# Which queues carry the two sliding layers' loads and the constant rows, and how many token buffers there are, in a four-layer attention kernel

## The chip, the cores and the metric

The kernel runs on one core of a Trainium2 chip. The core has a matrix engine (PE in the profile, with its weight loads shown apart as PEld), a vector engine (DVE), a scalar engine (ACT), a general engine (POOL) and an engine that only issues transfers (SP). Every engine works through its own instructions in order. ACT and POOL can issue DMA transfers from their own instruction streams too; a transfer that is issued so stands in line with the engine's other work. The metric is device time in microseconds (us) of one whole execution, as the median of several runs.

## The reference

```python
x = A_x                                             # 1 x 2048 tokens x 512, float32
x = x + A(layernorm(x), A_wqkv, A_wo)               # layer 0: sliding window of 256
x = x + B(layernorm(x), B_wqkv, B_wo)               # layer 1: full attention
x = x + A(layernorm(x), A_wqkv, A_wo)               # layer 2: as layer 0
x = x + B(layernorm(x), B_wqkv, B_wo)               # layer 3: as layer 1

# A and B, with 32 heads of 16
q, k, v = split(x @ wqkv)
p = softmax(q @ k.T / 4)          # A: only keys j with 0 <= i - j < 256
return (p @ v) @ wo
```

## The kernel before

The tokens are cut into four chunks of 512 (NQ = 4, QC = 512), and the 32 heads into eight groups of four (a group is `qd` in the code). For every layer, chunk and group the kernel makes scores on PE (line 675), exponentials of them on ACT (line 679), in the sliding layers sets the entries outside the window to zero on POOL (lines 742 and 745), and multiplies by the values on PE (line 719 in the full layers, 752 in the sliding ones). A sliding layer's group takes three steps, a full layer's sixteen. The product of one step is issued on PE two steps after its scores.

The work of projecting, normalizing and so on is called side work and is woven into the attention steps. `project` makes keys and queries (matmuls at line 387 in the sliding layers), ACT and DVE bring the result to two float16 halves (lines 495 and 498), and SP stores them to scratch tensors in DRAM (`kw` for sliding keys, `kf` for full keys, `qs` for queries; lines 508 to 512). A further row of each query, made on DVE as `m` or `m_None`, is stored at line 554. Other rows of these scratch tensors are constant ones or zeros; `fill` (lines 262 to 269) writes them. Before a group's scores, its part of the keys and queries is read back from DRAM: `load_win` (lines 700 to 709) for a sliding layer, with two transfers a group in the first chunk and three in the others, and `load_full` (lines 688 to 698) for a full one. The tiles that hold them, `kt` and `qt`, have three buffers each. A group's load is issued in the program one group before its use.

`load_x` (line 440) fetches four tiles of 128 tokens from DRAM into the tag `x`, which has XB buffers. In `wo` the result of the output projection is added to such a tile (line 617), the tile is stored (line 618) and its statistics and normalization follow on DVE (lines 406 to 432). The normalized tile `xh` is written transposed into `xc` by a transposing DMA on SP (line 453, `transposed`); the projections of the next layer read `xc`. `NN` does the same for the first layer's chunks 2 and 3 and `T` names the transposes. `weights` (line 348) fetches prepared weights from DRAM into two buffers.

The order on PE is written out by the program: the `Side` class decides with an estimated clock which piece of side work goes between which attention steps. The order on the other engines, SP and the issuing streams included, comes from the framework's scheduler, which places the instructions by priority and by when it expects them to be ready; the window's zeroing has a raised priority. The framework also chooses the semaphores. The trace names the semaphore on which each transfer's landing is counted: in this kernel eight of them serve all transfers, and SP and ACT take them in turn from the same eight. A transfer that is to use one waits until the transfer before it on that semaphore has landed, whichever of the two engines issued it.

`fill` is called at the start for chunk 0 (lines 1038 and 1039) and later through `F` (line 1071), a piece of side work, for the other chunks of layer 0 and for the scratch of the full layers. The calls through `F` make 21 transfers: two for each of the three key chunks and one for each of the three query chunks of the sliding layers, eight for the full layers' keys and four for their queries.

Of the kernel before, what the change touches and what calls it, by code (L numbers as in the profile page):

```python
# [18 lines left out]
S, D, H, DH, WIN = 2048, 512, 32, 16, 256  # L19
# [5 lines left out]
QC = 512  # L25
# [5 lines left out]
SCALE = DH ** -0.5  # L31
MM = 0.222
HEAD_START = 100
EB, XB, XNB, WB, VB, OB = 6, 5, 4, 2, 3, 5
RUN = 4
L_MIN = 2.0 ** -90
L_SUM = 2.0 ** 60
# [141 lines left out]
def interleave_kernel(tc, *args):  # L179
    nc = tc.nc  # L180
    with tc.tile_pool(name="flag", bufs=1) as fp:
        flag = fp.tile([1, 1], I32, name="flag")
        fast_path(tc, flag, *args)
        good = nc.values_load(flag, min_val=0, max_val=P)
        with tc.If(good < P):
            general_path(tc, *args)
# [3 lines left out]
def fast_path(ctx, tc, flag, a_x, a_wqkv, a_wo, b_wqkv, b_wo, out):  # L190
# [3 lines left out]
    nc = tc.nc  # L194
# [25 lines left out]
    def wait(us):  # L220
# [9 lines left out]
    ones = cp.tile([P, QC], F16, name="ones")  # L230
# [3 lines left out]
    zeros = cp.tile([P, QC], F16, name="zeros")  # L234
# [3 lines left out]
    kw = [dp.tile([NP, P, QC], F16, name=f"kw{c}") for c in range(NQ)]  # L238
    kf = dp.tile([NP, P, S], F16, name="kf")
    qs = {(ty, c): dp.tile([NP, P, QC], F16, name=f"qs{ty}_{c}") for ty in range(2) for c in range(NQ)}  # L240
# [11 lines left out]
                            fill=0.0, base=0, channel_multiplier=1)  # L252
    nc.gpsimd.affine_select(hsum, hsum, pattern=[[DH, 32]], compare_op=ALU.is_ge,
                            fill=0.0, base=DH - 1, channel_multiplier=-1)
# [4 lines left out]

    def fill(t, key, c0=0, c1=1):
        r4 = lambda d0, d1: rows(t).rearrange("h (d b) (c n) -> h d b c n", b=4, n=QC)[:, d0:d1, 3]
        for c in range(c0, c1):
            if key:
                nc.sync.dma_start(r4(0, 1)[:, 0, c], ones[:H])
                nc.sync.dma_start(r4(1, DH)[:, :, c], zeros[:H, None, :].broadcast_to([H, DH - 1, QC]))
            else:
                nc.sync.dma_start(r4(1, DH)[:, :, c], ones[:H, None, :].broadcast_to([H, DH - 1, QC]))


    def load_w(ty, s, tag="vf", n="wr", behind=None):
        raw = wp.tile([P, NC, D], F32, name=f"{n}{ty}_{s}", tag=tag, bufs=VB if tag == "vw" else NQ)
        if behind is not None:
            nc.vector.tensor_copy(raw[:, 0, :1], behind)
        if s < 3:
            nc.sync.dma_start(raw, mats[ty, s].rearrange("(k p) f -> p k f", p=P))
        else:

            for u in range(2):  # L280
                for h in range(4):
                    nc.sync.dma_start(raw[32 * h + DH * u:32 * h + DH * u + DH],
                                      mats[ty, s].rearrange("(k u h d) f -> u h d k f", u=2, h=4, d=DH)[u, h])
        return raw
# [413 lines left out]
        return kts, qt  # L698

    def load_win(l, c, qd):  # L700
        n = f"{l}_{c}_{qd}"
        kt = pp.tile([P, 2, S // 2], F16, name=f"kt{n}", tag="kt", bufs=3)
        qt = pp.tile([P, 2, QC], F16, name=f"qt{n}", tag="qt", bufs=3)
        pair = slice(2 * qd, 2 * qd + 2)
        nc.scalar.dma_start(qt, qs[0, c][pair].rearrange("r p n -> p r n"))
        nc.scalar.dma_start(kt[:, :, WIN:WIN + QC], kw[c][pair].rearrange("r p n -> p r n"))
        if c:
            nc.scalar.dma_start(kt[:, :, :WIN], kw[c - 1][pair, :, QC - WIN:].rearrange("r p n -> p r n"))
        return kt, qt

    def attn_full(l, c, qd, kt, qt, a):
# [323 lines left out]
    xs = load_x(0, 0)  # L1035
    xT = XC[0, 0] = wp.tile([P, 2, NC, QC], F16, name="xc0_0", tag="xc", bufs=NQ)
    raw = {m: load_w(0, m, "xc") for m in (1, 0, 2)}
    fill(kw[0], True)
    fill(qs[0, 0], False)
    for i in range(4):  # L1040
        stats(0, 0, i, xs[i])
    mv = ST[0, 0][1]
# [28 lines left out]
    def F(parts):  # L1071

        def gen():
            for p in parts:
                fill(*p)
                yield wait(8)
        return Work(gen(), 0.0, None, aside=True)
# [101 lines left out]
```

## Time and profile before

| | |
|---|---|
| median of three runs | 2735.25 us (2733.8 to 2735.88) |
| the profiled execution's own time | 2728.47 us |
| its span, first to last instruction | 2726.8 us |
| mean granted TensorE clock | 0.987 |
| PE busy | 2603.9 us, 95% |
| ACT busy | 2375.5 us, 87% |
| DVE busy | 852.7 us, 31% |
| POOL busy | 518.9 us, 19% |

All times inside the execution are us from the first instruction. Layer 0's attention runs from about 65 to 425 us, layer 1 from about 476, layer 2 from about 1440 to 1715, layer 3 from about 1760 to the end. A row of the timeline has the start, the duration, the engine, the line, the operation, the tile written and the tiles read, the shape and the count; in brackets the idle time of the engine before it and what ended it. An engine's name with a q (SPq, ACTq) is its issuing stream. A row of the waits has who waited, for whom, the total in us, how often, and the longest.

### The profile page before, as it was taken

How to read it: one execution, taken by the hardware profiler on the slowest of the kernel's cores; microseconds unless marked ns; L12 is line 12 of the kernel's file. 1: busy time of each engine (PE TensorE's matmuls, PEld its weight loads, DVE VectorE, ACT ScalarE, POOL GpSimd, SP SyncE). 2: the span in 40 equal slices, each digit the busy share in tenths (PEclk: the TensorE clock that was granted, in tenths of full speed). 3: DMA queues.
4: the chain of work that ended last, by engine and by line, in shares of the span. 5: the costliest groups of instructions: out<-in, count | busy, mean ns of one | idle time of the engine just before them, and what ended most of it. 6: DMA issues, size and time to landing. Idle time of an engine off the chain costs nothing.

```text
span 2726.8 us, 59387 instructions
## 1 busy us (share of the span) xinstructions
PE 2603.9 (95%) x24315; PEld 752.5 (28%) x24315; DVE 852.7 (31%) x1949; ACT 2375.5 (87%) x2683; POOL 518.9 (19%) x1154
## 2 busy tenths in 40 slices
PE   7798999999999999999999989899999999999998
PEld 3233344222222222222223333422222222222221
DVE  6565554013243113112216566311222221121111
ACT  4675664999999999999997767499999999999997
POOL 0465661000000000000006678100000000000000
PEclk9899999999999999999999999999999999999999
DMA  7898666234353223212325565523334333333331
GB/s 240 240 278 254 194 196 208 78 101 114 112 122 100 69 77 109 86 61 92 100 73 172 177 170 149 166 78 95 114 112 129 121 114 104 104 104 121 97 96 52
DMA packets 322715, 353.14 MB, mean 130 GB/s; under 512 B 114433, under 2 KB 234497, under 8 KB 316417
## 3 DMA queue, kind: packets, MB, share of 16 engines
q1 hardware_dynamic: 270336, 308.35, 37.3%
q10 hardware_dynamic: 52096, 40.91, 5.1%
q8 instruction: 192, 3.15, 0.5%
q14 instruction: 91, 0.74, 0.1%
HBM read 236.45 MB, written 96.99 MB: 122 GB/s over the span
## 4 chain that ended last, share of the span: by engine, by line
PE 77%; ACT 8%; DVE 7%; issue 5%; DMA 3%; SPq 1%; POOL 0%; ACTq 0%; DVEq 0%; POOLq 0%
PE acc L719 30%; PE s L675 20%; PE b L387 10%; PE acc L384 10%; ACT e L679 7%; PE acc L752 5%; PE bs L387 1%; DMA xc<-xh 1%; DVE ot L647 1%; DVE wa L321 1%; DVE xh L432 1%; DMA x<-in_A_x_dram 1%; DVE xn L426 0%; DVE xh L426 0%; DVE st L406 0%
## 5 line engine op out<-in xcount | busy, mean ns | idle before, releaser
L679 ACT ACTIVATE e<-s 128x1024 f32<-128x1024 f32 (+2 forms) x2432 | 2245.7, 1115 | 176.2 <-PE s L675 128.9
L719 PE MATMUL acc<-e,vt 128*17 128x512 f32 x8192 | 1080.4, 599 | 5.0 <-DVE ot L647 4.0
L675 PE MATMUL s<-qt,kt 64*128 64x512 f16 (+3 forms) x5504 | 771.4, 356 | 41.8 <-ACT e L679 23.2
L675 PEld LDWEIGHTS <-kt 64*128 64x128 f16 x5504 | 198.4, 94 | 785.6 <-issue 763.5
L745 POOL TENSOR_SCALAR_AFFINE_SELECT e<-e 128x256 f32<-128x256 f32 x512 | 231.2, 459 | 125.8 <-ACT e L679 124.9
L719 PEld LDWEIGHTS acc<-e,vt 128*17 128x17 f32 x8192 | 136.3, 95 | 385.6 <-issue 352.9
L647 DVE STREAM_TRANSPOSE ot<-acc 128x512 f32<-128x512 f32 x128 | 91.5, 715 | 447.9 <-PE acc L719 334.6
L742 POOL TENSOR_SCALAR_AFFINE_SELECT e<-e 128x256 f32<-128x256 f32 x448 | 196.9, 445 | 97.9 <-ACT e L679 94.0
L752 PE MATMUL acc<-e,vt 128*17 128x384 f32 (+2 forms) x2816 | 197.2, 395 | 0.0
L387 PE MATMUL b<-xc,w 128*128 128x512 f16 x676 | 164.4, 385 | 27.1 <-DMA xc<-xh 14.3
L663 POOL TENSOR_TENSOR oh<-o,oh 128x512 f16<-128x512 f32 x31 | 36.0, 1160 | 719.8 <-DVE oh L662 656.6
L387 PEld LDWEIGHTS <-w 128*128 128x128 f16 x800 | 72.5, 99 | 143.8 <-issue 61.2
L384 PE MATMUL acc<-xc,w_h 128*32 128x512 f16 x1296 | 108.5, 379 | 2.3 <-DVE km L536 2.3
L384 PE MATMUL acc<-xc,w 128*32 128x512 f16 x1344 | 108.9, 379 | 1.7 <-DVE sp L498 0.9
L604 POOL TENSOR_SCALAR vt<-vt 128x16 f32<-128x16 f32 (+1 forms) x96 | 24.5, 256 | 441.8 <-DVE vt L602 288.2
L497 DVE TENSOR_SCALAR sp_h<-acc 128x512 f16<-128x512 f32 x27 | 18.6, 690 | 282.0 <-PE acc L384 282.0
L635 DVE SCALAR_TENSOR_TENSOR x<-acc,x 128x512 f32<-128x512 f32 x60 | 41.5, 692 | 206.1 <-PE acc L384 206.1
L384 PE MATMUL acc<-wo,oh 128*32 128x512 f16 x1296 | 102.2, 382 | 3.3 <-DVE m_None L548 3.3
L497 DVE TENSOR_SCALAR sp<-acc 128x512 f16<-128x512 f32 x28 | 19.3, 688 | 270.7 <-PE acc L384 257.4
L503 POOL TENSOR_TENSOR sq_h<-sp_h 128x512 bf16<-128x512 f16 x27 | 28.1, 1040 | 388.5 <-DVE sp_h L497 388.5
L602 DVE COPY vt<-acc 128x256 f32<-128x256 f32 (+1 forms) x36 | 18.5, 514 | 264.3 <-PE acc L384 264.3
L387 PE MATMUL b<-wo,oh 128*128 128x512 f16 x390 | 97.0, 385 | 3.0 <-DMA wo<-wd 3.0
(134 smaller groups left out, 1537.8 us busy)
## 6 DMA issues: line engine op xcount, KB each, us to landing
kt<-kf SPq DMA_DIRECT2D x128, 512.0 KB
xd<-x SPq DMA_DIRECT2D x96, 256.0 KB
x<-xd SPq DMA_DIRECT2D x96, 256.0 KB
w<-wd SPq DMA_DIRECT2D x20, 1024.0 KB
kt<-kw ACTq DMA_DIRECT2D x64, 256.0 KB
qt<-qs ACTq DMA_DIRECT2D x64, 256.0 KB
qt<-qs SPq DMA_DIRECT2D x64, 256.0 KB
qs<-sp SPq DMA_DIRECT2D x48, 256.0 KB
```

The lines of the kernel that those rows point to most:

```text
L384: nc.tensor.matmul(ps[g:g + 32], a[:, g:g + 32], b, start=(i == 0), stop=(i == len(pairs) - 1), skip_group_check=True)
L387: nc.tensor.matmul(ps, a, b, start=(go and i == 0), stop=(i == len(pairs) - 1))
L497: nc.vector.tensor_scalar(sp[:, 0], ps, e, None, op0=ALU.mult)
L635: nc.vector.scalar_tensor_tensor(xs[i], ps, 1.0 / (UP[2] * UP[3]), xs[i], op0=ALU.mult, op1=ALU.add)
L647: nc.vector.transpose(ot.rearrange("p b r -> p (b r)"), a)
L663: (nc.gpsimd if l % 2 and (l, c, qd) != (3, NQ - 1, NQD - 1) else nc.vector).tensor_tensor(hl[:, 1], o, hl[:, 0], ALU.subtract)
L675: nc.tensor.matmul(ps[:, h, s0:s0 + wd_], kt[R * h:R * h + R, pr, kc:kc + P], qt[R * h:R * h + R, pr, qc:qc + wd_], start=True, stop=True)
L679: nc.scalar.activation(e[:, :, w0:w1], ps[:, :, w0:w1], AF.Exp, scale=SCALE)
L719: nc.tensor.matmul(a[32 * h:32 * h + DH + 1, :], V[l, qd // 4, j // 8][:, j % 8, 4 * (qd % 4) + h, :], es_[h // 2][:, h % 2, :], start=(j ...
L742: nc.gpsimd.affine_select(v, v, pattern=[[0, 2], [-1, P]], compare_op=ALU.is_gt, fill=0.0, base=0, channel_multiplier=1)
L745: nc.gpsimd.affine_select(v, v, pattern=[[0, 2], [1, P]], compare_op=ALU.is_ge, fill=0.0, base=0, channel_multiplier=-1)
L752: nc.tensor.matmul(a[32 * h:32 * h + DH + 1, q * P:(q + nb) * P], V[l, (4 * c + j) // 4][:, j % 4, 4 * qd + h, :], es_[h // 2][:, h % 2, s ...
```

## The change

Three things are changed. The loads of the sliding layers' keys and queries, which ACT issued in both, are issued by POOL in layer 0 and by SP in layer 2. The constant rows are written through POOL, apart from the two calls for chunk 0 at the start, which stay on SP. The tag `x` has six buffers where it had five.

```diff
-EB, XB, XNB, WB, VB, OB = 6, 5, 4, 2, 3, 5
+EB, XB, XNB, WB, VB, OB = 6, 6, 4, 2, 3, 5
...
-    def fill(t, key, c0=0, c1=1):
+    def fill(t, key, c0=0, c1=1, q=nc.gpsimd):
         r4 = lambda d0, d1: rows(t).rearrange("h (d b) (c n) -> h d b c n", b=4, n=QC)[:, d0:d1, 3]
         for c in range(c0, c1):
             if key:
-                nc.sync.dma_start(r4(0, 1)[:, 0, c], ones[:H])
-                nc.sync.dma_start(r4(1, DH)[:, :, c], zeros[:H, None, :].broadcast_to([H, DH - 1, QC]))
+                q.dma_start(r4(0, 1)[:, 0, c], ones[:H])
+                q.dma_start(r4(1, DH)[:, :, c], zeros[:H, None, :].broadcast_to([H, DH - 1, QC]))
             else:
-                nc.sync.dma_start(r4(1, DH)[:, :, c], ones[:H, None, :].broadcast_to([H, DH - 1, QC]))
+                q.dma_start(r4(1, DH)[:, :, c], ones[:H, None, :].broadcast_to([H, DH - 1, QC]))
...
     def load_win(l, c, qd):
-        n = f"{l}_{c}_{qd}"
+        n, q = f"{l}_{c}_{qd}", nc.sync if l else nc.gpsimd
         kt = pp.tile([P, 2, S // 2], F16, name=f"kt{n}", tag="kt", bufs=3)
         qt = pp.tile([P, 2, QC], F16, name=f"qt{n}", tag="qt", bufs=3)
         pair = slice(2 * qd, 2 * qd + 2)
-        nc.scalar.dma_start(qt, qs[0, c][pair].rearrange("r p n -> p r n"))
-        nc.scalar.dma_start(kt[:, :, WIN:WIN + QC], kw[c][pair].rearrange("r p n -> p r n"))
+        q.dma_start(qt, qs[0, c][pair].rearrange("r p n -> p r n"))
+        q.dma_start(kt[:, :, WIN:WIN + QC], kw[c][pair].rearrange("r p n -> p r n"))
         if c:
-            nc.scalar.dma_start(kt[:, :, :WIN], kw[c - 1][pair, :, QC - WIN:].rearrange("r p n -> p r n"))
+            q.dma_start(kt[:, :, :WIN], kw[c - 1][pair, :, QC - WIN:].rearrange("r p n -> p r n"))
         return kt, qt
...
-    fill(kw[0], True)
-    fill(qs[0, 0], False)
+    fill(kw[0], True, q=nc.sync)
+    fill(qs[0, 0], False, q=nc.sync)
```

## The prediction

> **What bounds the kernel now.** I read the page first, then who waited on PE, then the two sliding stages as windows, then the issuing streams around each stall.
>
> ```profile
> span 2726.8 us, 59387 instructions
> ...
> PE 2603.9 (95%) x24315; PEld 752.5 (28%) x24315; DVE 852.7 (31%) x1949; ACT 2375.5 (87%) x2683; POOL 518.9 (19%) x1154
> ...
> PE 77%; ACT 8%; DVE 7%; issue 5%; DMA 3%; SPq 1%; POOL 0%; ACTq 0%; DVEq 0%; POOLq 0%
> ```
>
> PE carries 77% of the chain. The change touches the two sliding layers, so only these two stretches can move (the sixth buffer reaches further, below):
>
> ```profile
> core 0: us, PE busy (x) PEld busy (x) DVE busy (x) ACT busy (x) POOL busy (x), PEclk, DMA share, GB/s
> 65.00:425.00 360.00, 322.89 (x2922) 127.12 (x2920) 202.18 (x473) 232.13 (x300) 207.66 (x496) 0.95 0.78 229
> 1440.00:1715.00 275.00, 256.61 (x2643) 98.32 (x2636) 172.04 (x418) 194.49 (x230) 200.15 (x490) 0.98 0.58 173
> ```
>
> In layer 0 PE is idle for 360 - 322.9 = 37.1 us and in layer 2 for 18.4 us. That is the most that better transfers can win. No other engine is full: POOL has 360 - 207.7 = 152.3 us left in layer 0. Which waits make up the 37 us:
>
> ```profile
> PE b L387 <- DMA xc<-xh: 14.3, 1, 14.3
> ...
> PE s L675 <- ACT e L679: 9.9, 10, 3.3
> PE b L387 <- DMA w<-wd: 9.9, 1, 9.9
> ```
>
> Two single stalls and ten small ones. The first is the largest. PE waits for the transposed tokens of chunk 2:
>
> ```profile
> 104.03 1.04 PE L387 MATMUL b<-w,xc 128*128 128x512 f16 x4
> 119.38 1.87 PE L387 MATMUL b<-xc,w 128*128 128x512 f16 x4 [14.31 <-DMA xc<-xh]
> ```
>
> DVE had the last of these tokens ready at 77.99 + 0.77 = 78.8 and the last query half that SP stores ahead of them at 84.28 + 0.69 = 85.0:
>
> ```profile
> 77.99 0.77 DVE L432 TENSOR_TENSOR xh<-xn,xh 128x512 f16<-128x512 f32 x1
> ...
> 84.28 0.69 DVE L498 SCALAR_TENSOR_TENSOR sp<-b,sp 128x512 f16<-128x512 f32 x1 [3.14 <-ACT sp L495]
> ```
>
> But SP issued the transposes from 101.28 to 117.25 only:
>
> ```profile
> 100.42 0.34 SPq L512 DMA_DIRECT2D qs<-sp  x1
> ...
> 101.28 4.59 SPq L453 DMA_TRANSPOSE xc<-xh  x2
> 105.98 2.76 SPq L554 DMA_DIRECT2D qs<-m_None  x4
> ...
> 110.20 0.43 SPq L269 DMA_DIRECT2D qs<-ones  x1
> 110.67 6.58 SPq L453 DMA_TRANSPOSE xc<-xh  x2
> ```
>
> What kept SP is in its own waits, from 60 to 310 us:
>
> ```profile
> SPq L511 <- DMA qt<-qs: 11.0, 3, 5.6
> ...
> SPq L512 <- DMA qt<-qs: 6.6, 1, 6.6
> SPq L282 <- DMA qt<-qs: 5.5, 1, 5.5
> ```
>
> A store of chunk 1's queries and a load of raw weights do not use the `qt` that ACT fetched. The link is the completion semaphore: SP and ACT take the same eight in turn, and the next user waits until the last one's transfer has landed. Since ACT issues its load only between exponentials, SP inherits ACT's lateness, 23.1 us in these three rows. The reverse holds too: ACT's loads wait for SP's transposes, and its exponentials stand behind them:
>
> ```profile
> 301.87 0.37 ACTq L706 DMA_DIRECT2D kt<-kw  x1
> 302.28 0.60 ACT L600 ACTIVATE vt<-b 128x512 f32<-128x512 f32 x1 [6.10 <-DMA xc<-xh]
> ```
> ```profile
> 161.06 0.49 PE L675 MATMUL s<-qt,kt 64*128 64x384 f16 x4 [2.10 <-ACT e L679]
> ```
> ```profile
> 303.84 0.39 PE L675 MATMUL s<-qt,kt 64*128 64x256 f16 x4 [3.30 <-ACT e L679]
> ```
> ```profile
> 1632.21 0.49 PE L675 MATMUL s<-qt,kt 64*128 64x256 f16 x4 [2.85 <-ACT e L679]
> ```
>
> These three are the largest of PE's waits for ACT in the two layers.
>
> **The change part by part.** *Layer 0's loads leave ACT.* ACT gives up 88 issues of layer 0 (two for each of 8 groups in chunk 0, three for each of 24) and with them the shared semaphores. Without ACT's loads ahead of them SP's last query store goes at about 86, the transposes follow. At the pace of the slower pair above (3.3 us each) four take 13 us, to about 99; the last landed 2 us after its issue ended (117.25 to 119.4), so at about 101. PE asks at 104.03 + 1.04 = 105.1. So the 14.3 us go, with 4 us to spare, and with them 0.8 us of the slow first matmuls (1.87 against 1.04 for four in the rows above). Bounds: -15.1 and 0, the latter if the saturated DMA engines bring the transposes as late as before; I take -15. The two waits for ACT in layer 0 go, 2.1 + 3.3 = -5.4. Late next after the first stall is the `w` load of the second:
>
> ```profile
> 240.48 0.35 SPq L445 DMA_DIRECT2D x<-in_A_x_dram  x1
> 240.92 0.38 SPq L348 DMA_DIRECT2D w<-wd  x1
> ```
>
> It stands on SP behind a token load that waits for a buffer until DVE's normalization; I leave its 9.9 us as they are.
>
> *They arrive on POOL.* There 88 loads and the 21 constant-row transfers become 109 issues in line with the window's zeroing:
>
> ```profile
> L745 POOL TENSOR_SCALAR_AFFINE_SELECT e<-e 128x256 f32<-128x256 f32 x256 | 116.8, 463 | 88.2 <-ACT e L679 87.8
> L742 POOL TENSOR_SCALAR_AFFINE_SELECT e<-e 128x256 f32<-128x256 f32 x224 | 100.6, 454 | 66.6 <-ACT e L679 64.8
> ```
>
> No POOL issue is in this trace. The nearest rows are ACT's issue (median 0.40 us, longest 2.20) and a full-tile operation on POOL (1.16 us):
>
> ```profile
> L706 ACTq DMA_DIRECT2D kt<-kw x64: 366/395/2202, 28.8 to 1683.3; - x64
> ```
> ```profile
> L663 POOL TENSOR_TENSOR oh<-o,oh 128x512 f16<-128x512 f32 x31 | 36.0, 1160 | 719.8 <-DVE oh L662 656.6
> ```
>
> I take 1.1 us, near the row of the same engine, and 0.4 and 2.2 as ends. 109 x 1.1 = 120 us against 152.3 idle, or 132 if 20 us of stalls vanish: it fits, nearly full. The zeroing is late by up to three issues in a row, 3.3 us. What hides that is the two-step distance between a score and its product; that PE hardly waits for POOL today shows in
>
> ```profile
> PEld acc L752 <- POOL e L742: 4.4, 18, 0.4
> ```
>
> At 0.25 us a group the remainder costs 32 x 0.25 = +8 us, an estimate. Ends: 0 at 0.4 us (44 us of issue, well hidden) and, at 2.2 us, 207.7 + 240 = 447 us of POOL in a stage of 360, +87.
>
> The page "SBUF — State Buffer" of the Trainium skill (its part on the two sides of SBUF) speaks against this move: descriptors for POOL's transfers are written by POOL's own cores, which VectorE's two-port operations lock out, 0.62 us alone becoming 3.1 us beside one. By an estimate from that page, 109 issues would cost 68 us alone, which fits, and 338 us if every one were so hit, which does not. The kinds of operation that the page names are few here: twenty normalizing passes of this form in the whole stage, 12.1 us together.
>
> ```profile
> L426 DVE TENSOR_SCALAR xn<-x,mv,y 128x512 f32<-128x512 f32 x20 | 12.1, 604 | 0.3
> ```
>
> So I expect few such hits; no issue of POOL's in this trace shows one.
>
> *Layer 2's loads go to SP.* ACT loses 88 issues of 0.4 us, all beside PE's work, and the 2.85 us at 1632 go: -3. SP takes 88 x 0.4 = 35 us of 275. What they now stand behind is a store that waits for DVE:
>
> ```profile
> SPq L618 <- DVE x L617: 79.7, 16, 13.4
> ```
>
> With three buffers a load may start when the group three before has made its scores, two groups ahead of its use. A group of three steps takes 275 / 32 = 8.6 us, so it has 17 us, and the longest wait of 13.4 still leaves 3.8 for 1.2 us of issue and 2 of landing. Where SP's chain is itself late, at the three inner chunk ends, some 1.2 us of issue come on top: between 0 and 4, I take +2.
>
> *Constant rows and the sixth buffer.* SP loses 21 issues of 0.4 us, in the first stall 0.43 us at 110.20; it is in the sum already. The sixth buffer lets one more token tile be fetched ahead, but a chunk has four and the fourth still waits for an older one to be normalized; 0, between -5 (the `w` load at 240.92 no longer behind it) and 0. In the full layers, where ACT is nearly always busy, it changes nothing.
>
> **The sum.** -15 - 5.4 + 8 - 3 + 2 = -13.4. The profiled execution took 2728.47, so 2715.1; it was 6.8 us below the median of the runs, 2735.25, against which the forecast stands: 2735.25 - 13.4 = 2722.
>
> **The rivals.** *POOL becomes the bound* (slower). Layer 0 holds POOL 207.7 us; with 109 issues it fills 360 us at (360 - 207.7) / 109 = 1.4 us each. Beyond that every 0.1 us costs 11 us. At 1.6 us, halfway from 1.16 to 2.2, POOL needs 382 us: +22, and 2757. For it: POOL works at 58% already, and each group's loads come in threes ahead of its zeroing. Against: the row of its own full-tile work is under 1.4.
>
> *The stall comes back* (no change). For it, the DMA engines are nearly full just there:
>
> ```profile
> 103.00:119.00 16.00, 2.07 (x20) 0.49 (x14) 2.65 (x6) 2.47 (x3) 3.05 (x7) 0.72 0.98 243
> 119.00:150.00 31.00, 28.79 (x240) 9.42 (x242) 25.86 (x61) 23.57 (x34) 20.18 (x44) 0.89 0.92 309
> 150.00:253.00 103.00, 88.95 (x792) 34.92 (x788) 56.34 (x127) 63.67 (x82) 56.17 (x135) 0.93 0.92 274
> ```
>
> The change moves no byte away; what PE gains at 105 it could lose by 253 to the same bytes. Then only the small waits remain to pay for POOL: -8.4 + 10 = +2, 2737. Against: at 243 GB/s the stall's stretch moved less than the next one's 309, so it was short of issue rather than of bandwidth. The page "DMA: Bandwidth & Descriptors" of the Trainium skill (its part "Issuing engines are not separate DMA queues") says that issuing from another engine saves only issue time; by it the change is worth nothing on PE's path, this rival's time. The trace's SP waits for `qt` say that here a queue also holds others up.
>
> *Layer 2's loads come late on SP.* The margin of 3.8 - 3.2 = 0.6 us is gone where a second store's wait, at the mean of 79.7 / 16 = 5.0 us, stands ahead of the same load: 4.4 us late, and once a chunk 4 x 4.4 = +18, so 2740. For it: SP's queue is in order, and the stores come four to a chunk. Against: their waits follow PE's own order, which the loads follow as well.
>
> **How the numbers follow.** The forecast has 0.58, POOL as the bound 0.22, the returning stall 0.12, late loads on SP 0.08. A measurement here tells 0.2%, 5.5 us, from no change. Faster is the forecast and a third of the returning stall: 0.62; same is the rest of that and half of the late loads: 0.12; slower 0.26. The forecast's own range is 2705 (all gains with the 5 us of the `w` load, POOL free: 2735 - 30) to 2730. For eight in ten it goes from 2703 up through most of the POOL rival, to 2762 (1.64 us an issue).
>
> **What would show it.** Right: no `DMA qt<-qs` among SP's waits in layer 0, transposes of chunk 2 issued before 95, PE's 14.3 us wait for `xc` gone, POOL's busy time in layer 0 up to about 330 us with issue rows near 1.1 us, and PE's idle time there at 25 us or less. Wrong: POOL issues over 1.4 us, PE's waits for POOL's zeroing of more than 1 us each, or SP's transposes still after 100. The prediction fails most easily in the price of one POOL issue.

## The result, and the profile after

The changed kernel took 2720.89 us (median of five runs, 2717.27 to 2722.7) against 2733.83 us (2730.97 to 2735.88) of the kernel before in the same comparison: a ratio of 0.9951 with a 95% interval of 0.9937 to 0.9966, or 13 us. A second comparison of the same two kernels gave 2719.3 against 2727.58 us, 0.9964 (0.9951 to 0.9977), or 8 us. The profiled execution after took 2722.56 us; the one before, 2728.47 us, was a low one, so the two traces differ by less than the medians do.

The head of the page after, and the two sliding stages as windows:

```profile
span 2720.6 us, 59477 instructions
...
PE 2599.0 (96%) x24315; PEld 751.6 (28%) x24315; DVE 859.3 (32%) x1949; ACT 2376.8 (87%) x2683; POOL 592.2 (22%) x1263
```
```profile
core 0: us, PE busy (x) PEld busy (x) DVE busy (x) ACT busy (x) POOL busy (x), PEclk, DMA share, GB/s
65.00:425.00 360.00, 325.87 (x2944) 128.78 (x2942) 202.62 (x456) 235.58 (x304) 265.52 (x586) 0.97 0.76 221
1440.00:1715.00 275.00, 258.18 (x2643) 99.18 (x2636) 175.72 (x420) 195.31 (x231) 202.89 (x490) 0.98 0.61 176
```

In layer 0 PE's idle time went from 37.1 to 360 - 325.9 = 34.1 us only, while POOL's work rose by 57.9 us to 265.5. In layer 2 the window hides the gain, because its fixed ends take in other work; the stage has to be cut at its own first and last product. That is the table to read this case by. Its times are the starts of rows of line 752 in each timeline, in us:

```
                         first product  layer 0  layers 0->2  layer 2  from there
                         of layer 0     to last  (layer 1)    to last  to the end
before                       70.7        352.7     1023.3      265.2     1014.9
after                        73.8        349.6     1022.6      258.7     1015.9
```

The first product came 3.1 us later, layer 0 took 3.1 us less, and so both end at 423.4 us: in this pair of traces all that was won in layer 0 was lost ahead of it. The 6.5 us of layer 2 make up the difference of the spans, 6.2 us. The last column holds the same instructions in every kernel, and over the fourteen traces of this case it took anything from 1013.6 to 1021.2 us; a few us between two spans therefore say little, and the columns of the sliding layers and the medians of many runs are what to go by.

What the prediction said of SP and of the first stall is there. SP's waits from 60 to 310 us no longer name `qt` or `kt`. The two longest groups are stores that wait for DVE's result and weight loads that wait for PE:

```profile
SPq L511 <- DVE sp L498: 33.0, 9, 10.8
SPq L348 <- PE s L675: 24.9, 4, 12.7
```

The trace shows the link itself too: in the changed kernel POOL's 109 transfers are counted on eight semaphores of their own, and no transfer of SP's or ACT's is counted on one of these. The transposes of chunk 2 go out from 89.41 us on instead of 101.28, and PE's wait there, 14.31 us before, is 2.26 (the profile names nothing that ended it):

```profile
89.41 7.13 SPq L453 DMA_TRANSPOSE xc<-xh  x2
96.65 3.04 SPq L554 DMA_DIRECT2D qs<-m_None  x4
...
100.13 7.13 SPq L453 DMA_TRANSPOSE xc<-xh  x2
```
```profile
110.90 1.02 PE L387 MATMUL b<-xc,w 128*128 128x512 f16 x4 [2.26 <-issue]
...
126.63 1.87 PE L387 MATMUL b<-xc,w 128*128 128x512 f16 x4 [5.33 <-DVE sp L498]
...
130.59 0.39 PE L675 MATMUL s<-qt,kt 64*128 64x256 f16 x2 [2.09 <-ACT e L679]
...
161.18 0.61 PE L675 MATMUL s<-qt,kt 64*128 64x128 f16 x4 [10.59 <-ACT e L679]
...
246.88 3.46 PE L387 MATMUL b<-xc,w 128*128 128x512 f16 x8 [4.49 <-DMA w<-wd]
```

But three new waits stand behind it, 5.33 + 2.09 + 10.59 = 18 us where there had been 2.1. The two of 2.09 and 10.59 us are for ACT. It was not held by a load of keys now, but by the preparation of layer 1's weights, which waits in ACT's order for raw weights, with the exponentials behind it:

```profile
127.66 2.19 ACT L290 ACTIVATE w<-wr 128x512 f16<-128x512 f32 x4 [8.27 <-DMA wr<-in_B_wqkv_dram]
...
159.07 1.15 ACT L290 ACTIVATE w<-wr 128x512 f16<-128x512 f32 x2 [8.54 <-DMA wr<-in_B_wqkv_dram]
```

SP issued these two loads at 111.96 and 145.50 us; before, the first was issued at 121.73, and ACT came to its tile at 132.27 without a wait. In the order that ACT now has, the preparation stands ahead of exponentials that could run, while its own data is not there. The wait of 5.33 us is another one. It is for DVE, whose line 498 stood behind statistics that waited for token loads:

```profile
121.30 0.69 DVE L406 BATCH_NORM_STATS2 st<-x 128x6 f32<-128x512 f32 x1 [2.54 <-DMA x<-in_A_x_dram]
...
125.95 0.63 DVE L498 SCALAR_TENSOR_TENSOR sp<-b,sp 128x512 f16<-128x512 f32 x1
```

POOL's issue is the term that the prediction was least sure of. By operation and tile (busy us, mean ns of one):

```profile
L705 POOL DMA_DIRECT2D qt<-qs x32 | 23.7, 740 | 23.2 <-PE s L675 14.6 <-DMA qs<-m_None 8.0 <-issue 0.3
L706 POOL DMA_DIRECT2D kt<-kw x32 | 23.2, 725 | 24.4 <-DMA kw<-sp 24.2
L708 POOL DMA_DIRECT2D kt<-kw x24 | 17.4, 725 | 0.0
```

0.73 us each, none over 0.79. PE's direct waits for the zeroing are small:

```profile
PE acc L752 <- POOL e L742: 2.7, 2, 2.1
```

### The profile page after: what moved, and what is told of

It is laid out like the page before. It is cut to its first block, busy times and chain, and to the rows that moved or that the text cites. A ratio compares the mean times of both kernels' runs of the same rounds, so it can differ in the third digit from the quotient of the medians.

```text
span 2720.6 us, 59477 instructions
## 1 busy us (share of the span) xinstructions
PE 2599.0 (96%) x24315; PEld 751.6 (28%) x24315; DVE 859.3 (32%) x1949; ACT 2376.8 (87%) x2683; POOL 592.2 (22%) x1263
## 4 chain that ended last, share of the span: by engine, by line
PE 77%; ACT 7%; DVE 6%; issue 4%; DMA 4%; SPq 1%; POOL 1%; ACTq 0%; DVEq 0%; POOLq 0%
PE acc L719 30%; PE s L675 20%; PE b L387 10%; PE acc L384 10%; ACT e L679 6%; PE acc L752 5%; DMA wr<-in_B_wqkv_dram 1%; PE bs L387 1%; DVE wa L321 1%; DVE ot L647 1%; DMA wr<-in_A_wqkv_dram 1%; DMA wo<-wd 1%; DVE xh L432 1%; DVE xn L426 0%; DMA w<-wd 0%
## 5 line engine op out<-in xcount | busy, mean ns | idle before, releaser
L503 POOL TENSOR_TENSOR sq<-sp 128x512 bf16<-128x512 f16 x28 | 29.1, 1041 | 367.1 <-DVE sp L497 367.1
```

Of the source, the lines that this page charges most:

```text
L503: nc.gpsimd.tensor_tensor(sq, sp[:, 0], sp[:, 0], ALU.mult)
```

## The experiments

Ratios are against the kernel before, run on the same chip in alternation; 0.001 is 2.7 us.

**One part alone.** The two moves of loads, the rows and the buffer were each made alone on the kernel before. Layer 2's loads alone:

```diff
-        nc.scalar.dma_start(qt, ...)            # and the two kt loads
+        q = nc.sync if l else nc.scalar
+        q.dma_start(qt, ...)
```

> Layer 2's loads alone go to SP; layer 0's loads stay on ACT, the constant rows on SP, five token buffers. By the prediction this is worth 1 us (-3 for the waits of ACT, +2 for SP). By the theory formed after the result, that ACT's hold-ups in layer 2 cost their whole stretch and not only PE's marked wait, it is worth 6 to 7 us, as layer 2 shortened by 6.5 us in the profile of the changed kernel. By the rival that layer 2's gain came from the token buffer or from a shifted start, it is worth 0 to 1 us.

0.9977 (0.9963 to 0.9991), 6 us, and the stage took 255.7 us: the theory formed after the result came out, and neither the prediction's 1 us nor the rival did. Layer 0's loads alone:

```diff
+        q = nc.scalar if l else nc.gpsimd
```

> Layer 0's loads alone go to POOL; layer 2's stay on ACT, the constant rows on SP, five token buffers. By the prediction 12 us are gained (-15 and -5.4 of stalls, +8 on POOL). By the theory formed after the result, that the freed stall comes back as waits for raw weights, the gain is between 0 and 5 us. By the rival that the constant rows at the start had spoiled a real gain here, it is 10 us or more, with PE starting its first attention step at about 70.7 us as before.

0.9972 (0.9960 to 0.9985), about 8 us, which lies between the expected values. The profiled execution shows more than that. In it layer 0's attention ran from 68.6 to 401.9 us and so ended 21.5 us sooner than in the kernel before. PE's wait for the transposes of chunk 2 was 2.59 us, and ACT waited 4.9 us for raw weights, not the 16.8 us of the changed kernel. So the freed stall need not come back. But this execution was the fastest of its twelve (2715.73 us, the median is 2723.03), and only 12.8 of the 21.5 us are left in its span; 5.7 of them are lost in the last stretch, whose instructions are the same. Why the median keeps so little of it is not shown. The constant rows alone:

```diff
-    def fill(t, key, c0=0, c1=1):
+    def fill(t, key, c0=0, c1=1, q=nc.gpsimd):   # chunk 0's two calls stay on SP
```

> The constant rows alone go through POOL. By the prediction 0 us. By the theory that POOL issues them at once and they crowd the first loads, 2 to 4 us slower, with the first attention step of layer 0 about 3 us later than 70.7. By the rival that SP's relief counts, 1 to 3 us faster.

1.0002 (0.9990 to 1.0013). And the sixth buffer alone:

```diff
-EB, XB, XNB, WB, VB, OB = 6, 5, 4, 2, 3, 5
+EB, XB, XNB, WB, VB, OB = 6, 6, 4, 2, 3, 5
```

> Six token buffers alone. By the prediction 0 us, at most 5 us faster if PE's wait for weights near 246 us shrinks because their load no longer stands behind a token load. By the rival that the buffer carries the whole gain, 8 to 13 us faster. In the full layers nothing moves by either.

1.0021 (1.0007 to 1.0035): it costs. So, by the medians, each move of loads is worth some 6 to 8 us, the rows nothing, and the buffer takes back 6.

**Parts put together or taken out of the changed kernel.** Both loads moved, rows on SP and five buffers as before:

```diff
-EB, XB, XNB, WB, VB, OB = 6, 6, 4, 2, 3, 5
+EB, XB, XNB, WB, VB, OB = 6, 5, 4, 2, 3, 5
...
-    def fill(t, key, c0=0, c1=1, q=nc.gpsimd):
+    def fill(t, key, c0=0, c1=1, q=nc.sync):
```

> Both loads moved as in the change, constant rows on SP and five token buffers as before. If the parts simply add, this is the sum of the two parts measured alone (ratios 0.9977 and 0.9972): 0.9949, -14 us, and the changed kernel (0.9951) owes the constant rows and the sixth buffer nothing. If the parts lean on each other, because the rows must leave SP when it takes over layer 2's loads, or the sixth buffer feeds the now earlier stage, this stays near one part alone, -8 us (0.997). If rows and buffer only cost (+5.7 us for the buffer alone), it is faster than the changed kernel by 5 us, 0.993.

0.9928 (0.9904 to 0.9952), as expected for the case that rows and buffer only cost. Only the second of these two edits, so six buffers and rows on SP:

> The changed kernel with its constant rows back on SP. Theory that the rows crowd the start: first attention step of layer 0 back from 73.8 us to about 70, the projecting and normalizing before it unchanged, and about 3 us faster than the changed kernel (0.994). Theory of the prediction, that the rows are worth nothing: within 1 us of the changed kernel (0.995). Theory that they hold SP up: 21 issues of 0.4 us, up to 9 us slower (0.998).

0.9985 (0.9975 to 0.9995). The first product is back at 68.4 us, as the theory of the crowded start has it, and the kernel is slower all the same; the sixth buffer is why, as the next pairs show. Only the first, so five buffers and rows on POOL:

> The changed kernel with five token buffers. If the buffer costs the same as alone (+5.7 us): 0.993. If it is worth nothing here, as predicted: 0.995. If it is what halved PE's wait for the weights at 247 us (9.9 to 4.5): that wait is 10 us again and the time 5 us longer, 0.997.

0.9969 (0.9958 to 0.9981). This is the number of the third expectation without its reason, for the wait for the weights is 4.9 us and not 10. With the loads moved, rows and buffer lean on each other, then:

```
                  five buffers             six buffers
rows on SP        0.9928 (and 0.9939)      0.9985
rows on POOL      0.9969                   0.9951 (and 0.9964): the changed kernel
```

The numbers in brackets are the second comparison, below. With the rows on SP the sixth buffer costs 0.5%; with the rows on POOL it costs nothing that can be told. The trace shows the place: layer 0 ends at 424.4 us with six and at 417.4 with five, 7 of the 12 us between the medians of these two kernels. SP's stream ahead of the `w` load that PE waits for at about 245 us, with six buffers and with five (both with the rows on SP, the loads moved):

```profile
237.24 0.34 SPq L618 DMA_DIRECT2D xd<-x  x1
242.56 0.35 SPq L445 DMA_DIRECT2D x<-in_A_x_dram  x1
243.00 0.38 SPq L348 DMA_DIRECT2D w<-wd  x1
```
```profile
237.73 0.34 SPq L618 DMA_DIRECT2D xd<-x  x1
238.17 0.38 SPq L348 DMA_DIRECT2D w<-wd  x1
244.51 3.93 SPq L445 DMA_DIRECT2D x<-in_A_x_dram  x3
```

With six, a token load stands ahead of the weights and holds them to 243.00; with five they leave at 238.17. PE's waits are, with six and with five:

```profile
249.79 2.74 PE L387 MATMUL b<-xc,w 128*128 128x512 f16 x6 [12.91 <-DMA w<-wd]
```
```profile
243.93 2.31 PE L387 MATMUL b<-xc,w 128*128 128x512 f16 x5 [5.45 <-DMA w<-wd]
```

The same wait was 9.92 us before, and 14.29 with the sixth buffer alone:

```profile
249.93 3.33 PE L387 MATMUL b<-xc,w 128*128 128x512 f16 x8 [14.29 <-DMA w<-wd]
```

In the changed kernel it is 4.49 with six and in the one with five 4.9: with the rows off SP no token load stands there, and the buffer is harmless.

**The rows and the start.** The first product of layer 0 starts at 70.7, 69.1, 68.6, 70.2, 68.4, 67.2 and 68.3 us in the seven kernels whose rows go through SP (before; layer 2's loads alone, layer 0's alone, the buffer alone; rows back on SP; both loads twice). With the rows on POOL it starts at 73.8, 74.7, 76.7, 74.1 and 73.7 (the changed kernel twice, five buffers, and the two experiments with doubled issues and halved weights), at 82.4 with the rows alone and at 81.9 with all loads on SP. No value of one group reaches the other; the means lie 5.7 us apart even without the last two. The first 68 us of before, of the changed kernel, and of both loads alone in its second run:

```profile
0.00:68.00 68.00, 51.92 (x237) 23.63 (x238) 42.47 (x104) 28.19 (x48) 4.76 (x20) 0.97 0.77 240
```
```profile
0.00:68.00 68.00, 48.70 (x218) 22.29 (x218) 46.77 (x117) 25.35 (x43) 15.64 (x35) 0.95 0.95 283
```
```profile
0.00:68.00 68.00, 52.15 (x250) 24.05 (x252) 44.41 (x114) 30.49 (x51) 10.03 (x28) 1.00 0.82 247
```

(Engines as above, then the granted clock, the share of the DMA engines, GB/s.) POOL is idle at the start, so the rows of chunks 1 and 2 go out at once, from 2.33 us on, and the DMA engines are 95% busy instead of 77%. All the rows below are of the changed kernel:

```profile
2.33 0.70 POOL L266 DMA_DIRECT2D kw<-ones  x1
...
5.96 0.66 POOL L269 DMA_DIRECT2D qs<-ones  x1
```
```profile
9.67 6.86 SPq L269 DMA_DIRECT2D qs<-ones  x1
16.57 7.00 SPq L445 DMA_DIRECT2D x<-in_A_x_dram  x4
```

Before, the row of 9.67 began at 6.47 and took 2.44 us, and the tokens left at 8.96. What PE then waits for is the tokens of chunk 1. Their four transposes are issued by ACT in all these kernels, not by SP. The last of the four and the product behind it, before and in the changed kernel:

```profile
48.10 1.27 ACTq L453 DMA_TRANSPOSE xc<-xh  x1
...
51.45 4.44 PE L387 MATMUL bs<-xc,w 128*128 128x512 f16 x12 [2.05 <-DMA xc<-xh]
```
```profile
49.78 2.68 ACTq L453 DMA_TRANSPOSE xc<-xh  x1
...
55.82 4.47 PE L387 MATMUL bs<-xc,w 128*128 128x512 f16 x12 [5.35 <-DVE st L406]
```

The profile puts the second wait down to statistics on DVE, but the product reads none; the semaphores on which PE waits there are those of ACT's transposes, and with the rows on POOL and five buffers the same wait, 7.9 us, is put down to `xc`. So this product comes 4.4 us later, and the first product of the attention 3.1.

**Is POOL needed?** The changed kernel with all loads on SP:

```diff
-        n, q = f"{l}_{c}_{qd}", nc.sync if l else nc.gpsimd
+        n, q = f"{l}_{c}_{qd}", nc.sync
```

> The changed kernel with layer 0's loads on SP too, none on POOL. If what helps is that ACT no longer shares its semaphores with SP and its exponentials stand behind no load, POOL is not needed: 0.995, with the 14 us wait for the transposes gone as in the changed kernel. If SP's order matters (loads behind stores that wait for DVE, transposes behind loads), PE waits for `kt` and `qt` in layer 0, several times 2 to 5 us, and it comes to 0.998 or more. If POOL's issues cost PE the 8 us of the prediction, it is 0.992.

0.9994 (0.9983 to 1.0005): the whole gain is gone. Two of PE's waits in its trace, one ahead of layer 0's attention and one in it:

```profile
61.81 1.44 PE L387 MATMUL bs<-xc,w 128*128 128x512 f16 x3 [9.02 <-DMA qs<-m_None]
...
116.41 0.82 PE L675 MATMUL s<-qt,kt 64*128 64x384 f16 x4 [6.85 <-DMA kt<-kw]
```

The second is the kind that was expected: SP issued this `kt` load at 112.93 us only, behind two stores and a transpose that took its stream from 100.98 to 111.78 us. The first is of another kind. The product reads `xc` and `w`, and the store that the profile names only shares a semaphore with one of ACT's transposes of chunk 1, the last of which took ACT until 59.66 us here and until 52.46 in the changed kernel. The first product of the attention comes 8.1 us later than in the changed kernel (81.9 against 73.8), the end of layer 0 9.0 us later (432.4 against 423.4): most of the loss lies ahead of the attention, and why those transposes were later is not shown.

So taking the loads off ACT is not enough; on SP they cost as much as they bring, on POOL they do not. The page "DMA: Bandwidth & Descriptors" of the Trainium skill ("Issuing engines are not separate DMA queues") says that another issuing engine saves only issue time. This pair, 0.3 to 0.4% apart with the same bytes, shows that the engine that issues can decide whether a change pays. How much of it is the place in the stream, and how much SP's own issue time (88 loads at 0.36 us or more), is not shown.

**What does a POOL issue cost?** Each load of layer 0 cut in two by its two parts, so 176 issues in place of 88 for the same bytes:

```diff
-        q.dma_start(qt, qs[0, c][pair]...)               # and the two kt loads
+        for r in [slice(None)] if l else [slice(0, 1), slice(1, 2)]:
+            q.dma_start(qt[:, r], qs[0, c][pair][r]...)
```

> The changed kernel with each of layer 0's loads split by its two parts: 176 issues on POOL in place of 88, the same bytes. At 0.72 us an issue POOL is busy 63 us more, about 329 of layer 0's 360 us. By the prediction's price (8 us for 120 us of issue) +4 us against the changed kernel. If the two steps' distance between scores and product hides it all: 0 to 1 us. If POOL is near its bound already: +10 us or more, and PE's waits for POOL's zeroing above 3 us each.

0.9977 (0.9967 to 0.9986), 4 to 7 us more than the changed kernel's two results; the interval of the second of these, 0.9951 to 0.9977, overlaps. Half a load takes POOL 0.55 us, not 0.72:

```profile
L706 POOL DMA_DIRECT2D qt<-qs x64 | 35.4, 554 | 14.6 <-PE s L675 13.0 <-issue 1.4
```
```profile
65.00:425.00 360.00, 330.54 (x2957) 130.02 (x2956) 213.38 (x459) 236.01 (x305) 295.84 (x669) 0.97 0.78 223
```

So POOL worked 30 us more, to 296 of 360 us. PE's direct waits for the zeroing are 0.7 and 0.6 us in this trace, and its layer 0 ends at 422.2 us, within the changed kernel's 421.2 to 423.4. The medians suggest that more issues cost; the trace does not show where.

**The raw weights.** The changed kernel with half of layer 1's raw key, query and value weights loaded and that half used twice, so it leaves out the other half:

```diff
-            nc.sync.dma_start(raw, mats[ty, s]...)
+            u = 2 if ty and n == "wr" else NC
+            nc.sync.dma_start(raw[:, :u], mats[ty, s]...[:, :u])
```

> The changed kernel, but of layer 1's raw key, query and value weights only the first half is loaded and used twice (this leaves out part of the computation). If ACT's 16.8 us of waits for them in layer 0 come from how long the loads take beside everything else (13 to 16 us each), they go, with them PE's waits of 10.6 and 5.3 us for ACT and DVE, and the kernel is 10 us or more faster than the changed one (0.991 against before). If the loads are issued too late, half of ACT's wait stays and the gain is 5 us. If the gain of layer 0 is limited by something else, it goes to the next wait and the time stays at 0.995.

0.9944 (0.9929 to 0.9959), beside 0.9951 and 0.9964. In layer 0's part of the trace (its lines are one further down):

```profile
PE s L676 <- ACT e L680: 13.3, 11, 4.1
...
ACT w L291 <- DMA wr<-in_B_wqkv_dram: 4.3, 1, 4.3
```

ACT's wait fell from 16.8 to 4.3 us. That does not single out how long the loads take, since the order moved too: SP issued the three loads at 112.60, 125.54 and 130.73 us, where the changed kernel has 111.96, 127.52 and 145.50. The first wait was halved (8.27 to 4.34 us) with a load that was issued at nearly the same time; the second one went, with a third load issued 15 us sooner. PE's longest wait for ACT fell from 10.6 to 4.1, but its sum from 16.2 to 13.3 only, and layer 0 ended at 419.7 us, 1.5 to 3.7 us sooner. The expected 10 us did not come: other small waits took the place of the large one. The single row of 10.59 us is thus not worth 10.59. PE's wait of 5.33 us went as well, but it was for DVE, behind token loads.

**The best combination beside the changed kernel.** Both once more, on one chip:

> The changed kernel once more, beside the two moved loads alone, on one chip. If its first ratio holds: 0.995. If the difference to the two loads alone came from the chips or from the scatter of the runs, the two are within 0.1% of each other here.

> Both loads moved, constant rows on SP, five token buffers, once more. If rows and buffer cost as the stages say (first attention step 67 against 74 us), it is 5 us faster than the changed kernel, 0.993 against before. If the earlier difference was scatter: 0.995.

The changed kernel took 2719.3 us, 0.9964 (0.9951 to 0.9977); the two loads alone 2712.68, 0.9939 (0.9924 to 0.9955). The two loads alone lead by 0.0025 in the ratio here and led by 0.0023 in the first runs, which were two separate comparisons; the intervals overlap a little each time, the sign is the same. By its ratio it is the fastest kernel tried, with a first product at 67.2 and 68.3 us where the changed kernel has 73.8 and 74.7.

## Why the prediction was right, and where its steps were not

The time was 2720.89 against 2722 forecast, faster as forecast, and the direction is right for the reason given first: ACT's loads and SP's stores held each other up, and this hold-up went. But the steps do not have the sizes that were given to them; several errors cancel, and that the sum came out within 2 us is luck. Two signs that the prediction had set for itself came out against it: PE's idle time in layer 0 is 34.1 us and not 25 or less, and the last transposes of chunk 2 were still being issued after 100 us.

*The stall for `xc`, -15 us.* The mechanism is shown by SP's waits and by the 14.31 us that became 2.26. Two details failed. The four transposes did not begin at 86 us but at 89.41, and the second pair was issued from 100.13 to 107.26, since four stores of line 554 stand between the pairs for 3 us, as they did before; there were no 4 us to spare. And in the changed kernel the gain did not stay: 12.7 us of waits behind ACT's weight preparation and 5.3 us behind DVE's statistics followed within 50 us. The forecast named the `w` load as what is late next and missed these. With layer 0's loads moved alone, ACT waited little for raw weights, and layer 0 ended 21.5 us sooner in that trace.

*PE's waits for ACT in layer 0, -5.4 us.* One of the two waits went, the 3.30 us at 303.84. Wrong as a sum: in the first 480 us PE waited 9.9 us in ten such places before (the row in the prediction) and 16.2 us in eight after.

*POOL, +8 us.* 109 issues at 0.52 to 0.79 us raised POOL's busy time by 592.2 - 518.9 = 73.3 us, not 120, and 57.9 of them lie in layer 0. POOL did not become the bound: 265.5 of 360 us. The rival that it would, at over 1.4 us an issue, is refuted. The page "SBUF — State Buffer" of the Trainium skill (its part on the two sides of SBUF) gives 0.62 us for a transfer of POOL's alone and 3.1 us beside a two-port operation of VectorE. That is a whole transfer and not the issue, and no row here shows such a lock-out: in the changed kernel no issue held POOL for more than 0.79 us. What POOL's part costs PE stays open. PE's direct waits are 2.7 us, the waits of its weight loads for line 742, 4.4 us in the prediction's row, are 8.8, and 30 us of added issue made 4 to 7 us.

*Layer 2, -3 + 2 us.* The right mechanism, and too small by 4 to 6 us. In the four profiled kernels with these loads on ACT the stage took 265.2 to 266.6 us; in the ten with them on SP 255.7 to 260.0; the means lie 7.9 us apart. In this stage of the changed kernel neither PE nor its weight loads waited for a transfer ahead of a score for more than 0.8 us, so the +2 and that rival fall. The -3 had counted PE's idle time at 1632 only. What held ACT there is a `kt` load, with the exponentials behind it:

```profile
1630.62 0.39 ACTq L708 DMA_DIRECT2D kt<-kw  x1
1631.14 1.94 ACT L679 ACTIVATE e<-s 128x1024 f32<-128x1024 f32 x2 [5.17 <-DMA xc<-xh]
```

The stretch around it, cut in the trace of before:

```profile
1628.00:1632.20 4.20, 1.36 (x12) 0.40 (x5) 3.18 (x10) 1.06 (x2) 0.47 (x2) 1.00 1.09 231
1632.20:1637.00 4.80, 4.37 (x31) 1.50 (x31) 1.29 (x5) 3.20 (x4) 3.89 (x11) 0.64 0.79 198
1637.00:1642.00 5.00, 5.00 (x58) 1.87 (x57) 2.30 (x5) 3.87 (x5) 2.93 (x8) 1.00 0.41 88
```

Behind the 2.85 us of idle the granted clock is 0.64 for 4.8 us, which is 4.8 x 0.36 = 1.7 us more. Over the whole stage, cut at its own ends, before and after:

```profile
1446.70:1711.90 265.20, 248.24 (x2566) 95.11 (x2566) 165.56 (x396) 190.61 (x224) 197.85 (x485) 0.98 0.58 169
```
```profile
1446.00:1704.70 258.70, 246.39 (x2569) 94.81 (x2566) 167.65 (x396) 190.99 (x224) 200.60 (x485) 0.99 0.60 173
```

The same 2566 weight loads belong to 16.96 us of idle before and 12.31 after, -4.65, and to 1.85 us less of busy PE at the better clock: 6.5 together. The waits that went are ACT's hold-up at 1632 and part of one for `wv` (5.11 us before at 1582, 3.64 after).

*Constant rows, 0.* Their sum is about 0 when they are moved alone, but not because they cost nothing: the start is 12 us late (82.4 against 70.7) and the rest of layer 0 is shorter by as much (339.5 against 352.7). The transposes of chunk 2 do not come sooner by it, SP issues them from 99.39 to 118.34 us. PE only gets to them later, so most of the late start goes where the stall was; a wait of 7.27 us for ACT is left there, and the `w` wait is 4.55 us instead of 9.92. Beside the moved loads no such stall is left to take in the late start, and the cost shows: with five buffers 0.9969 against 0.9928.

*Sixth buffer, 0, between -5 and 0.* The sign was wrong. One more token load placed ahead of the `w` load holds that back; +0.2% alone. In the changed kernel the moved rows undo this, and the `w` wait, which the forecast left at 9.9 us, was 4.5.

*The sum.* Where layer 0 ends takes in start and stage. It was 423.4, 426.7 and 428.5 us in the three kernels without the rows or layer 0's loads moved (mean 426.2; the last has the sixth buffer, and without it the mean is 425.1) and 423.4 and 421.2 in the changed kernel's two traces (422.3): about -3 to -4. Layer 2 adds -6.5 and -5.2 against 265.2. These make about -9 to -10, between the measured 13 and 8. The forecast had -12.4 for layer 0 and -1 for layer 2, so in the changed kernel the larger half came from the part that was thought small. The rival that the stall comes back was right in part: the stall for `xc` did not come back, but most of its gain was lost again, to a crowded start and to loads that were late for ACT and DVE.

## What to carry to other kernels

Price a wait by its idle time and by the slower clock behind it, and look for what stands next in the in-order queue of each engine the wait had also delayed; one long row in a trace does not measure what its removal brings: the row of 2.85 us stood in a stage that became 6.5 us shorter, and when the row of 14.31 us was gone, the changed kernel's layer 0 ended only 3 to 4 us sooner. A transfer moved into an idle queue starts at once (the rows here from 2.33 us on), and at the start of a kernel that means beside the loads that everything waits for. Try the parts of a change singly and together: the cost of the rows was hidden by the stall that the moved loads removed, and the sixth buffer was harmless only beside the moved rows.

## What the runs showed of the hardware

After a long wait PE is granted half its clock for about 4 us. Before's windows behind the two large stalls:

```profile
119.30:124.00 4.70, 4.62 (x20) 1.10 (x20) 0.51 (x1) 1.51 (x2) 1.32 (x4) 0.53 0.99 307
124.00:130.00 6.00, 6.00 (x54) 2.10 (x52) 5.72 (x21) 4.25 (x6) 1.99 (x6) 1.00 1.03 400
```
```profile
245.90:250.00 4.10, 4.07 (x14) 1.47 (x16) 0.20 (x1) 0.00 (x0) 0.00 (x0) 0.50 1.03 222
250.00:255.00 5.00, 5.00 (x56) 1.90 (x53) 3.50 (x9) 4.61 (x6) 1.92 (x6) 1.00 0.90 211
```

That is, by an estimate from these rows (4.7 x 0.47 and 4.1 x 0.50), some 2 us on top of each, where the forecast had 0.8 for the first and nothing for the second. The page "TensorE: Matmul & The Clock Gate" of the Trainium skill (Part 1) states a half clock after about 3.4 us without work, lifted after about 3.4 us of work; the two rows are near it, with half a clock for some 4 us. The wait of 2.85 us in layer 2 is shorter than that, and its clock still fell, to 0.64 over the next 4.8 us.

An issue on POOL costs by the pattern, not by the bytes: 0.725 us for `kt` loads of 256 KB and the same 0.725 us for those of 128 KB, which have as many rows of half the length, but 0.55 us where a load has half the rows. By these two, an estimate, 0.38 us are fixed and 0.35 us go with the rows of a whole load.

The engine that issues a load also decides how it is cut. From 65 to 425 us the loads of layer 0 are 22304 packets for 18.36 MB when ACT issues them, and 5792 packets for the same 18.36 MB when POOL does (layer 0's loads alone). Their share of the DMA engines' time is about the same, 17.7% and 16.5%, so the larger packets save no time of the DMA engines.
